# Reordering the opening stage of a fused polynomial-sketch attention and SwiGLU kernel

## The chip, the cores and the metric

One core of a Trainium2 chip. The metric is device time in microseconds (us) of one execution. The five engines of the core run their own instruction lists in order: TensorE (PE in the profile; its weight loads are PEld), VectorE (DVE), ScalarE (ACT), GpSimd (POOL) and SyncE (SP, which only issues DMAs). A letter q behind an engine's name stands for its sequencer.

## The reference

Attention without softmax over 4 batches, 4 heads, 1088 positions, 32 values per head, then a SwiGLU block over the 4352 tokens:

```
phi(x) = outer(S1 x, S2 x)                 # 8 x 8 = 64 features per position
kv  = sum over s of phi(k) v               # 64 x 32 per head
z   = sum over s of phi(k)                 # 64 per head
attn = (phi(q) kv) / (phi(q) z + 1e-6)
x    = attn, heads side by side            # 4352 x 128
out  = (silu(x w_gate) * (x w_val)) w_out  # d_ff = 1536
```

q, k and v are float32. [...]

## The kernel before

**The long part.** x is kept transposed in SBUF, 128 features by 4352 tokens, cut into 12 blocks of 384 or 320 tokens (three per batch). A *unit* (L646) is one block against one of 12 slices of 128 hidden columns: two matmuls (gate and value, L651), a silu on ACT (L657) and a product on DVE (L665). `down` (L673) is the third matmul (L679). Units fill the span from about 17 us to the end, and the attention of later batches is slipped in between them.

**The opening.** Before the first unit, the attention of batch 0 has to give the first block of x, and the first slices of the weights have to be narrowed. The order of every engine's instructions is the order of the lines in the source; nothing reorders them. The opening is L720 to L844:

- Loads. SP issues S1, k (544 KB), the first third of q, four pieces of v, later the second third of q, the second pieces of the gate and value weights, and the last third of q. ACT issues S2 and the first weight pieces. I call the pieces of the gate weights wg0 (128 columns), wg1 (256 columns), wg2 and so on, those of the value weights wv0, wv1, wv2. The DMAs take eight completion semaphores in turn, in the order of the source. A DMA whose semaphore still belongs to an earlier DMA first waits, on its engine, for that earlier one to land. So the fourth piece of v waits for k, as the two share a semaphore.
- Sketches. `s12` and `sq` (L755 to L762) are S1 and S2 laid out for the matmuls.
- Keys. `turn_k` transposes k on DVE in three pieces (L263), `key_products` (L278) multiplies with S1 and S2, `key_copy` brings a product from PSUM to SBUF on ACT (L295, or L292 for the last piece), and `key_features` (L301) forms the 64 features `phk`. The first two pieces' features are made by DVE, the last one's by POOL.
- `unit_sums` (L324) adds the features over the positions (z, then `zq`), `key_values` (L312) multiplies them with v (kv, then `kvs`). `turn_sums` (L343) and `turn_kv` (L335) turn both round into `kvz`.
- Queries, by thirds of the batch (`steps`): `turn_q` (L269), `query_products` (L368), `query_copy` on ACT (L384, L387), `query_features` on DVE (L398, L404; one instruction where a product has a two-bank buffer, two where it has two single banks).
- `totals` (L420) gives denominators (`which=(1,)`) and numerators (`which=(0,)`), `divide` (L433) transposes the denominators (`dT`, L441), inverts them (`rc`), spreads them (`rd`, L449) and writes x (`xT`, L466).
- Narrowing. `narrow` (L199) works in three steps, which `part(name, i)` calls one at a time: L217 and L218 on DVE; L222 and L223 on ACT; L225 and L229 on DVE followed by a multiplication on POOL (L238; of wg1 and wv1, half of it on DVE), and then the issue of a further weight load by SP. Four raw buffers hold 64-bit pieces, so a further load waits until the raw data of an earlier piece has been read.
- `keep_warm` (L189) runs matmuls without use for their result, to keep PE busy.

PSUM has four single banks, g0, g1, g2 and acc, and two two-bank buffers, a and b.

Of the kernel before, what the change touches and what calls it, by code (L numbers as in the profile page):

```python
# [19 lines left out]
def kernel(  # L20
# [28 lines left out]
    nc = tc.nc  # L49
    P = nc.NUM_PARTITIONS  # L50
    B, H, S, Dh = q.shape
# [3 lines left out]
    NX = S // 32  # L55
    HX = NX // 2
    NC = (NX + 3) // 4
    F = R * R
# [7 lines left out]
    XS = plan[0]  # L66
# [21 lines left out]
    def bank(tag=None):  # L88
        if tag is None:
            tag = free_banks[turn[0] % len(free_banks)]  # L90
            turn[0] += 1
        return psum.tile([P, TB], FP32, tag=tag, name="bank")

    def wide(tag):
        return psum.tile([P, 2, TB], FP32, tag=tag, name=tag)
# [6 lines left out]
    wide_w = moe_w_gate.dtype == I64  # L102
# [12 lines left out]
    NRAW = 4  # L115
# [6 lines left out]
    def load_q(b, x0=0, x1=NX):  # L122
        src = q[b].rearrange("h (pp x) d -> (h pp) x d", pp=32)
        nc.sync.dma_start(out=qld[:, x0:x1, :], in_=src[:, x0:x1, :])
# [14 lines left out]
    def load_next(queue=nc.sync):  # L139
        if not coming:  # L140
            return
        name, i = coming.pop(0)
        dst, src = weights[name]
        c0, c1 = pieces[name][i]
        if name == "wo":
            part = src.rearrange("(c p) d -> p c d", p=P)[:, c0:c1, :]
        else:
            part = src.rearrange("p (c f) -> p c f", f=P)[:, c0:c1, :]
        if not wide_w:
            queue.dma_start(out=dst[:, c0:c1, :], in_=part)  # L150
            return
        t = raw[name, i] = stage.tile([P, 3, P], I64, tag="raw", name="raw", bufs=NRAW)
        queue.dma_start(out=t[:, 0 : c1 - c0, :], in_=part)
# [114 lines left out]
    def turn_q(x0, n):  # L268
        nc.vector.transpose(  # L269
            out=qT[:, 2 * x0 : 2 * x0 + 2 * n, :],  # L270
            in_=qld[:, 2 * x0 : 2 * x0 + 2 * n, :],
        )
# [13 lines left out]
    def key_copy(ps, c0, c1, aside=False):  # L286

        n = c1 - c0
        ab = ps[:, 0 : 64 * n].rearrange("p (x t r) -> p x t r", t=2, r=R)
        if aside:  # L290
            kab = apool.tile([P, n * H, 2, R], FP32, tag="kab", name="kab")
            nc.scalar.copy(kab[:], ab)  # L292
            return kab[:, :, 0, :], kab[:, :, 1, :]
        ka = apool.tile([P, n * H, R], FP32, tag="ka%d" % c0, name="ka")
        nc.scalar.copy(ka[:], ab[:, :, 0, :])  # L295
        return ka[:], ab[:, :, 1, :]

    def key_features(phk, prod, c0, c1, engine=nc.vector):
        ka, kb = prod
        n = (c1 - c0) * H  # L300
        engine.tensor_tensor(  # L301
            out=phk[:, c0:c1, :, :, :].rearrange("p c h i j -> p (c h) i j"),
            in0=ka.unsqueeze(3).to_broadcast([P, n, R, R]),
            in1=kb.unsqueeze(2).to_broadcast([P, n, R, R]),
            op=ALU.mult,
        )

    def key_values(kv, phk, c0, c1):

        for c in range(c0, c1):  # L310
            for h in range(H):
                nc.tensor.matmul(  # L312
                    kv[32 * h : 32 * h + 32, 0:F],
                    vld[:, h, c, :],
                    phk[:, c, h, :, :].rearrange("p i j -> p (i j)"),
                    start=(c == 0),
                    stop=(c == NC - 1),
                )

    def unit_sums(kz, phk, c0, c1):  # L320

        for c in range(c0, c1):
            a = c % 4
            nc.tensor.matmul(  # L324
                kz[32 * a : 32 * a + 32, 0 : H * F],
                ones[:, 0:Dh],
                phk[:, c, :, :, :].rearrange("p h i j -> p (h i j)"),
                start=(c < 4),
                stop=(c + 4 >= NC),
            )  # L330

    def turn_kv(kvs, kzp):
# [18 lines left out]
    def query_products(x0, n, tags):  # L351

        w = 32 * n
        pss = []
        for pr in range(2):
            if isinstance(tags[pr], str):
                both = wide(tags[pr])[:].rearrange("p g (t w) -> p g t w", t=2)
                parts = [both[:, g] for g in range(2)]
            else:
                both = None  # L360
                parts = [
                    bank(t)[:].rearrange("p (t w) -> p t w", t=2) for t in tags[pr]
                ]
            for t in range(2):
                for half in range(2):
                    for g in range(2):
                        r = slice(64 * pr + 32 * g, 64 * pr + 32 * g + 32)
                        nc.tensor.matmul(  # L368
                            parts[g][F * half : F * half + F, t, 0:w],
                            sq[r, t, :, :].rearrange("p i j -> p (i j)"),  # L370
                            qT[r, 2 * x0 : 2 * x0 + 2 * n, :].rearrange(
                                "p (x a) t -> p a x t", a=2
                            )[:, half],
                            start=True,
                            stop=True,
                        )
            pss.append((both, parts))
        return pss

    def query_copy(n, both, parts):  # L380
        w = 32 * n
        qb = apool.tile([P, 2, 32 * XS], FP32, tag="qb", name="qb", bufs=2)
        if both is not None:
            nc.scalar.copy(qb[:, :, 0:w], both[:, :, 1, 0:w])  # L384
        else:
            for g in range(2):
                nc.scalar.copy(qb[:, g, 0:w], parts[g][:, 1, 0:w])  # L387
        return qb
# [40 lines left out]
    def side_by_side(tag):  # L429
        both = wide(tag)[:].rearrange("p g (t w) -> p g t w", t=2)  # L430
        return both[:, :, 0, :], both[:, :, 1, :]
# [292 lines left out]
    def part(name, i):  # L724

        next(fills[name, i], None)
# [3 lines left out]
    if wide_s:  # L730
# [1 line left out]
        steps_s = narrow(s32[:], sraw[:], [2 * R, Dh])  # L732
        next(steps_s)
        next(steps_s)
    for _ in range(2):
        load_next(nc.scalar)
    load_q(0, 2 * XS, 4 * XS)
    for _ in range(2, NRAW if wide_w else len(coming) + 2):
        load_next()
    load_q(0, 4 * XS, NX)  # L740
    run(steps_s)
    srep = bank("g0")
    for h in range(H):
# [16 lines left out]
    )  # L760
    nc.scalar.copy(sq[:, 0, :, :], sTv[:, 0, :].unsqueeze(2).to_broadcast([P, R, R]))
    nc.scalar.copy(sq[:, 1, :, :], sTv[:, 1, :].unsqueeze(1).to_broadcast([P, R, R]))  # L762
    for c in fpieces:
        turn_k(*c)
    prods = []
    for t, c in zip(("g1", "g2", "acc"), fpieces):
        ps = bank(t)
        key_products(ps, *c)
        prods.append(key_copy(ps, *c, aside=(c[1] == NC)))
    phk = apool.tile([P, NC, H, R, R], FP32, tag="phk", name="phk")  # L770
    kz, kv = bank("g0")[:, 0 : H * F], wide("b")[:, 0, 0:F]
    n = steps[0][1]
    key_features(phk, prods[0], *fpieces[0])
    unit_sums(kz, phk, *fpieces[0])
    turn_q(*steps[0])
    pss = query_products(*steps[0], ("a", ("g1", "acc")))
    qbs = [query_copy(n, *pss[0])]
    key_features(phk, prods[1], *fpieces[1])
    unit_sums(kz, phk, *fpieces[1])
    key_features(phk, prods[2], *fpieces[2], engine=nc.gpsimd)  # L780
    unit_sums(kz, phk, *fpieces[2])
    part("wg", 0)
    part("wv", 0)
    zq = apool.tile([P, H * F], FP32, tag="zq", name="zq")
    kvs = apool.tile([P, F], FP32, name="kvs0")
    kvz = [apool.tile([P, P], FP32, name=x) for x in ("kvz0", "kvz1")]
    qbs.append(query_copy(n, *pss[1]))
    nc.scalar.copy(zq[:], kz)
    key_values(kv, phk, *fpieces[0])
    phq = query_features(n, pss, qbs, pairs=(0,))  # L790
    query_features(n, pss, qbs, phq=phq, pairs=(1,))
    turn_q(*steps[1])
    ps = bank("g0")
    turn_sums(zq, sel[:], ps)
    nc.scalar.copy(kvz[1][:], ps[:, 0:P])
    part("wg", 0)
    key_values(kv, phk, *fpieces[1])
    nd = [bank(t) for t in ("g2", "acc")], side_by_side("a")[0]
    totals(n, phq, kvz, nd, which=(1,))
    key_values(kv, phk, *fpieces[2])  # L800
    nc.scalar.copy(kvs[:], kv)
    ps = bank("g1")
    turn_kv(kvs[:], ps)
    nc.scalar.copy(kvz[0][:], ps[:, 0:P])
    part("wv", 0)
    totals(n, phq, kvz, nd, which=(0,))
    pss = query_products(*steps[1], ("b", ("g0", "g1")))
    qbs = [query_copy(steps[1][1], *ps) for ps in pss]
    turn[0] = 2
    keep_warm(3, ps=wide("a")[:, 0, :])  # L810
    divide(0, *steps[0], nd, among=("wg", "wv"))

    att = attention(1, ((0, 3), (3, NC)))
    for _ in range(2):
        part("wg", 1)
        part("wv", 1)
    unit(0, 0, late=True)
    phq = query_features(steps[1][1], pss, qbs)  # L820
    part("wg", 1)
    part("wv", 1)
    nd = totals(steps[1][1], phq, kvz, side_by_side("b"))
    unit(0, 1, late=True)
    divide(0, *steps[1], nd)
    part("wg", 2)
# [113 lines left out]
```

## Time and profile before

| | us |
|---|---|
| median of 4 runs (lowest, highest) | 311.71 (311.44, 312.49) |
| the profiled execution's own time | 311.97 |
| its span in the profile | 310.2 |
| PE busy in the span | 302.5 |
| DVE / ACT / POOL busy | 176.3 / 96.0 / 37.2 |

Busy time by stage, us:

| stage | length | PE | DVE | ACT | POOL |
|---|---|---|---|---|---|
| 0 to 6.40 | 6.40 | 4.73 | 1.57 | 2.05 | 2.46 |
| 6.40 to 16.89 | 10.49 | 9.18 | 8.90 | 4.51 | 2.34 |
| 16.89 to 25 | 8.11 | 7.49 | 7.90 | 5.11 | 1.21 |
| 25 to 35 | 10.00 | 10.00 | 7.90 | 7.61 | 4.92 |
| 35 to 60 | 25.00 | 24.83 | 23.72 | 13.21 | 9.11 |
| 60 to 300 | 240.00 | 240.00 | 124.48 | 62.57 | 17.13 |

The profile shows one execution. A row of its timeline gives the start, the length, the engine, the line, what is written from what, and in brackets how long the engine had been idle and what ended that. The chain of waits goes back from the last instruction to what released each step; its rows give start, length and what ran. Busy time of PE is modelled at its matmuls' ends, and successive instructions of an engine overlap by some hundredths of a us, so that steps are best counted from start to start.

### The profile page before, as it was taken

To read this page: it belongs to the slowest core of one execution; us is meant where nothing else is said; L and a number is where in the kernel's file an instruction comes from. 1 tells how busy PE (TensorE), PEld (TensorE's weight loads), DVE (VectorE), ACT (ScalarE), POOL (GpSimd) and SP (SyncE) were. 2 spreads that over 40 slices of the span, in tenths; PEclk is the share of its full clock that TensorE was granted. 3 is DMA by queue.
4 is the path that set the end of the run, shared out by engine and by line. 5 is a ranking of instruction groups with operands and counts; after the bars stand their busy time and mean duration, and the time that the engine had idled before them with its cause. 6 is when DMAs were issued, how large, how long until landed. Compare 5 with 4: busy or idle time off the path is not lost.

```text
span 310.2 us, 5154 instructions
## 1 busy us (share of the span) xinstructions
PE 302.5 (97%) x2068; PEld 191.0 (62%) x2068; DVE 176.3 (57%) x333; ACT 96.0 (31%) x228; POOL 37.2 (12%) x54
## 2 busy tenths in 40 slices
PE   7899999999999999999999999999999999999994
PEld 6445555656565556666666666655676656676664
DVE  3797999752758655369944552897522323333321
ACT  3457666232102223132222232222222222222230
POOL 3225322335000001500000033000000000000000
PEclk9999999999999999999999999999999999999998
DMA  7564291402211021120100100100010100100101
GB/s 189 138 184 121 63 311 45 146 0 56 44 27 21 2 97 49 25 74 0 26 2 0 22 3 2 19 6 0 8 20 0 21 2 1 25 0 1 23 0 25
DMA packets 24663, 13.96 MB, mean 45 GB/s; under 512 B 18368, under 2 KB 22720, under 8 KB 24640
## 3 DMA queue, kind: packets, MB, share of 16 engines
q1 hardware_dynamic: 23712, 13.28, 16.9%
q10 hardware_dynamic: 928, 0.36, 0.6%
q8 instruction: 16, 0.26, 0.4%
q14 instruction: 7, 0.06, 0.1%
HBM read 11.41 MB, written 2.23 MB: 44 GB/s over the span
## 4 chain that ended last, share of the span: by engine, by line
PE 87%; DVE 7%; ACT 2%; DMA 1%; issue 1%; SPq 0%; DVEq 0%
PE bank L651 50%; PE bank L679 28%; DVE hj L665 2%; DMA kld<-in_k_dram 1%; DVE exp L225 1%; PE a L602 1%; PE a L278 1%; PE a L312 1%; PE b L278 1%; DVE exp L217 1%; DVE man L229 1%; PE a L693 1%; PE a L528 1%; ACT exp L222 1%; PE bank L324 1%
## 5 line engine op out<-in xcount | busy, mean ns | idle before, releaser
L665 DVE TENSOR_TENSOR hj<-sg,bank 128x384 f32<-128x384 f32 (+1 forms) x138 | 72.7, 529 | 102.3 <-PE bank L651 101.3
L657 ACT ACTIVATE sg<-bank 128x384 f32<-128x384 f32 (+1 forms) x144 | 67.7, 472 | 155.9 <-PE bank L651 155.8
L651 PE MATMUL bank<-xT,wg 128*128 128x384 f32 (+1 forms) x288 | 112.9, 474 | 0.2 <-DVE wg L238 0.2
L651 PE MATMUL bank<-xT,wv 128*128 128x384 f32 (+1 forms) x288 | 111.6, 469 | 0.4 <-DVE wv L238 0.4
L679 PE MATMUL bank<-hj,wo 128*128 128x384 f32 (+2 forms) x288 | 105.3, 460 | 0.2 <-DVE hj L665 0.2
L651 PEld LDWEIGHTS bank<-xT,wv 128*128 128x128 f32 x288 | 54.2, 190 | 34.5 <-DVE hj L665 2.6
L679 PEld LDWEIGHTS bank<-hj,wo 128*128 128x128 f32 x288 | 54.4, 190 | 32.9 <-issue 0.8
L651 PEld LDWEIGHTS bank<-xT,wg 128*128 128x128 f32 x288 | 53.1, 190 | 32.0 <-issue 2.6
L474 POOL TENSOR_TENSOR zs<-phk 128x1024 f32<-128x1024 f32 x3 | 7.1, 2352 | 111.9 <-PE bank L651 104.2
L565 DVE TENSOR_REDUCE dot<-phq 128x96 f32<-128x768 f32 x9 | 13.8, 1532 | 0.0
L301 DVE TENSOR_TENSOR phk<-kas,a 128x512 f32<-128x512 f32 (+1 forms) x12 | 8.7, 749 | 5.2 <-ACT kas L509 5.2
L707 DVE STREAM_TRANSPOSE o<-bank 128x384 f32<-128x384 f32 (+2 forms) x12 | 6.6, 549 | 6.9 <-PE bank L679 6.6
L222 ACT ACTIVATE exp<-exp,rebias 128x384 int32<-128x384 int32 (+3 forms) x15 | 8.3, 555 | 4.9 <-DVE exp L217 4.2
L589 DVE STREAM_TRANSPOSE phT<-phq 128x768 f32<-128x768 f32 x9 | 8.7, 968 | 0.1
L301 DVE TENSOR_TENSOR phq<-qab 128x768 f32<-128x768 f32 x9 | 8.6, 951 | 0.0
L558 DVE TENSOR_TENSOR phq<-zrep,qab 128x768 f32<-128x768 f32 x9 | 8.5, 942 | 0.0
L225 DVE SCALAR_TENSOR_TENSOR exp<-raw,exp 128x384 int32<-128x384 int32 (+2 forms) x14 | 7.7, 547 | 0.0
L620 ACT COPY xT<-a 128x64 f32<-128x64 f32 (+4 forms) x9 | 2.4, 332 | 15.9 <-PE b L602 9.5
L217 DVE TENSOR_SCALAR exp<-raw 128x384 int32<-128x384 int32 (+2 forms) x14 | 6.6, 474 | 0.6 <-DMA raw<-in_moe_w_val_dram 0.6
L229 DVE SCALAR_TENSOR_TENSOR man<-raw,man 128x384 f32<-128x384 uint32 (+2 forms) x14 | 6.9, 491 | 0.0
L223 ACT ACTIVATE man<-man 128x384 f32<-128x384 int32 (+3 forms) x15 | 6.8, 453 | 0.0
L263 DVE STREAM_TRANSPOSE kT<-kld 128x384 f32<-128x384 f32 (+2 forms) x9 | 6.1, 692 | 0.7 <-DMA kld<-in_k_dram 0.7
(113 smaller groups left out, 162.7 us busy)
## 6 DMA issues: line engine op xcount, KB each, us to landing
kld<-in_k_dram SPq DMA_DIRECT2D x4, 544.0 KB, 4.5
vld<-in_v_dram SPq DMA_DIRECT2D x12, 144.0 KB, 5.2
qld<-in_q_dram SPq DMA_DIRECT2D x3, 544.0 KB, 3.3
raw<-in_moe_w_out_dram SPq DMA_DIRECT2D x4, 384.0 KB, 4.2
out_dram<-o SPq DMA_DIRECT2D x28, 48.0 KB, 1.8
raw<-in_moe_w_gate_dram SPq DMA_DIRECT2D x3, 384.0 KB, 3.2
raw<-in_moe_w_val_dram SPq DMA_DIRECT2D x3, 384.0 KB, 3.2
out_dram<-o SPq DMA_DIRECT2D x16, 40.0 KB, 1.7
```

What stands on the lines that cost most here:

```text
L217: nc.vector.tensor_scalar(e[:], hi, 0x7FF00000, None, op0=ALU.bitwise_and)
L222: nc.scalar.activation(e[:], e[:], AF.Relu, bias=rebias[: shape[0], :], scale=8.0)
L225: nc.vector.scalar_tensor_tensor(out=e[:], in0=hi, scalar=-(1 << 31), in1=e[:], op0=ALU.bitwise_and, op1=ALU.bitwise_or,)
L229: nc.vector.scalar_tensor_tensor(out=f, in0=lo, scalar=2.0**-52, in1=f, op0=ALU.mult, op1=ALU.add)
L301: engine.tensor_tensor(out=phk[:, c0:c1, :, :, :].rearrange("p c h i j -> p (c h) i j"), in0=ka.unsqueeze(3).to_broadcast([P, n, R, R]), i ...
L558: nc.vector.tensor_tensor(out=prod, in0=zrep[:].unsqueeze(1).to_broadcast([P, n, H * R, R]), in1=fac.unsqueeze(3).to_broadcast([P, n, H * ...
L565: nc.vector.tensor_reduce(out=dot[:, x, :], in_=phq[:, c0:c1, :, :, :].rearrange("p c h i j -> p (c h) j i"), axis=AX.X, op=ALU.add,)
L589: nc.vector.transpose(out=phT[:, :, :, c0:c1, :].rearrange("p h g c t -> p c (h g) t"), in_=phq[:, c0:c1, :, :, :].rearrange("p c h (g i) ...
L651: nc.tensor.matmul(o[:, 0:n], w[:, j, :], xT[:, t0 : t0 + n], start=True, stop=True)
L657: nc.scalar.activation(sg[:, 0:n], g[:, 0:n], AF.Silu)
L665: nc.vector.tensor_tensor(out=hj[:, 0:n], in0=sg[:, 0:n], in1=u[:, 0:n], op=ALU.mult)
L679: nc.tensor.matmul(acc[i][:, 0:n], wo[:, j, :], hidden[i, j][:, 0:n], start=(j == 0), stop=(j == NCH - 1),)
```

## The change

Only the opening is changed. Of the three pieces of keys, POOL's (now called `aside`) is transposed, multiplied and copied first, and its features are added as the second of the three. The first third's query products come right behind the key products on PE, into the two two-bank buffers a and b, and the transpose of that third of q goes ahead of the key features on DVE; the query features follow the key features. kv is gathered in the single bank acc, in the order first, POOL's, second piece. The two weight loads of ACT are issued behind its copies of the sketches, and they and the rest of the loads come later in the source, so that the eight semaphores are dealt out anew: of the four pieces of v none waits for another DMA any more, the second third of q waits for S2 as before, and the load of wv0 now waits for k. The first narrowing step of wg1 comes ahead of `divide`, its last step ahead of the query features of the second third, and the first step of wv1 behind them. `keep_warm(3)` becomes `keep_warm(1)`. From `part("wg", 2)` on, the instructions are the same.

```diff
@@ key_values, unit_sums @@
-    def key_values(kv, phk, c0, c1):
+    def key_values(kv, phk, c0, c1, order=range(NC)):
...
-                    start=(c == 0),
-                    stop=(c == NC - 1),
+                    start=(c == order[0]),
+                    stop=(c == order[-1]),
...
-    def unit_sums(kz, phk, c0, c1):
+    def unit_sums(kz, phk, c0, c1, order):
...
             a = c % 4
+            same = [x for x in order if x % 4 == a]
...
-                start=(c < 4),
-                stop=(c + 4 >= NC),
+                start=(c == same[0]),
+                stop=(c == same[-1]),
@@ the opening @@
-    for _ in range(2):
-        load_next(nc.scalar)
-    load_q(0, 2 * XS, 4 * XS)
-    for _ in range(2, NRAW if wide_w else len(coming) + 2):
-        load_next()
-    load_q(0, 4 * XS, NX)
     run(steps_s)
...
     nc.scalar.copy(sq[:, 1, :, :], sTv[:, 1, :].unsqueeze(1).to_broadcast([P, R, R]))
-    for c in fpieces:
+    for _ in range(2):
+        load_next(nc.scalar)
+    load_q(0, 2 * XS, 4 * XS)
+    for _ in range(2, NRAW if wide_w else len(coming) + 2):
+        load_next()
+    load_q(0, 4 * XS, NX)
+
+    c0, c1, aside = fpieces
+    order = [c for p in (c0, aside, c1) for c in range(*p)]
+    for c in (aside, c0, c1):
         turn_k(*c)
-    prods = []
-    for t, c in zip(("g1", "g2", "acc"), fpieces):
+    prods = {}
+    for t, c in zip(("acc", "g1", "g2"), (aside, c0, c1)):
         ps = bank(t)
         key_products(ps, *c)
-        prods.append(key_copy(ps, *c, aside=(c[1] == NC)))
+        prods[c] = key_copy(ps, *c, aside=(c == aside))
+    turn_q(*steps[0])
+    n = steps[0][1]
+    pss = query_products(*steps[0], "ab")
+    qbs = [query_copy(n, *ps) for ps in pss]
     phk = apool.tile([P, NC, H, R, R], FP32, tag="phk", name="phk")
-    kz, kv = bank("g0")[:, 0 : H * F], wide("b")[:, 0, 0:F]
-    n = steps[0][1]
-    key_features(phk, prods[0], *fpieces[0])
-    unit_sums(kz, phk, *fpieces[0])
-    turn_q(*steps[0])
-    pss = query_products(*steps[0], ("a", ("g1", "acc")))
-    qbs = [query_copy(n, *pss[0])]
-    key_features(phk, prods[1], *fpieces[1])
-    unit_sums(kz, phk, *fpieces[1])
-    key_features(phk, prods[2], *fpieces[2], engine=nc.gpsimd)
-    unit_sums(kz, phk, *fpieces[2])
-    part("wg", 0)
-    part("wv", 0)
+    kz = bank("g0")[:, 0 : H * F]
+    key_features(phk, prods[aside], *aside, engine=nc.gpsimd)
+    for c in (c0, c1):
+        key_features(phk, prods[c], *c)
+    for c in (c0, aside, c1):
+        unit_sums(kz, phk, *c, order)
...
-    qbs.append(query_copy(n, *pss[1]))
     nc.scalar.copy(zq[:], kz)
-    key_values(kv, phk, *fpieces[0])
-    phq = query_features(n, pss, qbs, pairs=(0,))
-    query_features(n, pss, qbs, phq=phq, pairs=(1,))
+    kv = bank("acc")[:, 0:F]
+    key_values(kv, phk, *c0, order)
+    phq = query_features(n, pss, qbs)
+    part("wg", 0)
+    part("wv", 0)
     turn_q(*steps[1])
+    part("wg", 1)
     ps = bank("g0")
     turn_sums(zq, sel[:], ps)
     nc.scalar.copy(kvz[1][:], ps[:, 0:P])
     part("wg", 0)
-    key_values(kv, phk, *fpieces[1])
-    nd = [bank(t) for t in ("g2", "acc")], side_by_side("a")[0]
-    totals(n, phq, kvz, nd, which=(1,))
-    key_values(kv, phk, *fpieces[2])
+    key_values(kv, phk, *aside, order)
+    den = side_by_side("a")[0]
+    totals(n, phq, kvz, ([None] * 2, den), which=(1,))
+    key_values(kv, phk, *c1, order)
     nc.scalar.copy(kvs[:], kv)
...
     part("wv", 0)
+    part("wg", 1)
+    nd = [bank(t) for t in ("g2", "acc")], den
     totals(n, phq, kvz, nd, which=(0,))
...
-    keep_warm(3, ps=wide("a")[:, 0, :])
+    keep_warm(1, ps=wide("a")[:, 0, :])
     divide(0, *steps[0], nd, among=("wg", "wv"))
...
-    for _ in range(2):
-        part("wg", 1)
-        part("wv", 1)
     unit(0, 0, late=True)
+    part("wg", 1)
     phq = query_features(steps[1][1], pss, qbs)
-    part("wg", 1)
+    part("wv", 1)
     part("wv", 1)
     nd = totals(steps[1][1], phq, kvz, side_by_side("b"))
+    part("wv", 1)
     unit(0, 1, late=True)
```

## The prediction

> **What bounds the kernel.** First the page: PE is busy for nearly the whole span.
>
> ```profile
> PE 302.5 (97%) x2068; PEld 191.0 (62%) x2068; DVE 176.3 (57%) x333; ACT 96.0 (31%) x228; POOL 37.2 (12%) x54
> PE 87%; DVE 7%; ACT 2%; DMA 1%; issue 1%; SPq 0%; DVEq 0%
> ```
>
> What PE lacks to the span is 7.7 us, half of it at the end. So the opening can only win by letting PE begin its steady work earlier. Where it begins is read from the chain of waits of the first 30 us:
>
> ```profile
> 1.28 4.48 DMA kld<-in_k_dram
> 5.79 1.50 DVE kT L263 x3
> ...
> 10.89 0.18 issue
> 11.07 0.54 PE b L312 x24
> 11.61 0.59 PE bank L343 x16
> ...
> 15.43 0.60 DVE xT L466 x2
> ...
> 20.49 0.30 DVE wv L238
> 20.79 0.14 issue
> 20.93 3.69 PE bank L651 x10
> ```
>
> k lands at 5.76; PE and ACT carry the chain to 15.43; then DVE alone carries it to 20.79, and PE waits for the second slice of the value weights until 20.93. From there PE's units follow with few holes (10.00 busy of 10.00 in 25 to 35, 24.83 of 25 in 35 to 60). From `part("wg", 2)` on the instructions are the same, so what DVE's end of wv (20.79) gains, the whole rest should gain. DVE is nearly full too (23.72 of 25), but with the same work behind the same point it shifts as a whole.
>
> **Step 1, features.** The waits, of the engines and of SP's queue, tell why PE stood at 10.89 (who waited for whom, us in total, times, longest):
>
> ```profile
> PEld b L312 <- DMA vld<-in_v_dram: 0.6, 1, 0.6
> SPq L130 <- DMA kld<-in_k_dram: 2.2, 1, 2.2
> ```
>
> SP held the last piece of v for 2.2 us until k had landed, issued it at 5.78, and 5.2 later (page's landing for that form in the DMA view) it was there: 10.98. And the sums before it (L324) ended at 10.89, as POOL's features came last:
>
> ```profile
> 8.51 1.51 POOL L301 TENSOR_TENSOR phk<-kab 128x768 f32<-128x768 f32 x1 [4.86 <-ACT kab L292]
> 8.67 0.92 DVE L301 TENSOR_TENSOR phk<-ka,bank 128x768 f32<-128x768 f32 x1
> ```
>
> After: POOL's copy is ACT's first, 7.03 + 0.32, and POOL runs from about 7.51 to 9.02 instead of to 10.02. DVE does the same three instructions between 7.28 and the end of its features (transpose of q 0.57, features 0.95 and 0.92), only in another order: it ends at about 9.55, as now at 9.59. ACT's copies of the other products stay where PE's products put them (7.49, 8.03). PE's query products (0.93 from 8.97 to 9.90) fill 8.0 to 8.93, when PE now waits for features; their cover is that hole. Then the sums: two groups early, the last six matmuls at 9.55 + 0.15 for 0.63 (the first six of now, 8.41 to 9.04): 10.35 against 10.89. `zq` follows on ACT at 10.40 for 0.37, against 10.94; `turn_sums` (L343), which waits for it, starts at about 10.82 against 11.54: **-0.72**, if v lies there by about 10.3, so that the first `key_values` (0.47 to the next start) is out of the way. From there to `xT` PE and ACT do the same things (second and third group change places): `xT` starts at 15.41 - 0.72 = 14.69.
>
> **Step 2, DVE before `divide`.** `dT` could start at 13.27 - 0.72 = 12.55. DVE has 0.19 of room behind it (`rd` ends at 15.18, `xT` waits for PE to 15.41). In front of it now stand, behind the query features (two instructions of 0.55, the first from 9.47, when ACT has copied its product, so that they end at 10.49, where three end at 12.15 now): wg0's and wv0's first step, the transpose of q, and, new here, wg1's first step. From the landing of wv0 to `dT` that is 0.15 + 0.13 + 0.49 + 0.20 + 0.20 = 1.17 from start to start (rows of 10.79 to 12.07 and of 17.05 to 17.45). So wv0 must land by 12.55 + 0.19 - 1.17 = **11.57**, or DVE, whose list is in order, holds `dT`, and PE behind it, by what is over.
>
> **Step 3, loads.** wv0 lands at 10.77 now (issued by ACT at 3.19, 7.6 later). After the change ACT issues wg0 at 5.44 and wv0 at about 5.85, past k's landing, so that its new wait costs nothing; the kab copy behind it on ACT is not due before 7.03. SP issues v's last piece at about 3.6 instead of 5.78 and q's second third at about 4.1 instead of 6.13; wg1 and wv1 still wait for q's first third and v's first piece to land. The bytes are the same 2.46 MB, all landed by 12.99 now, so values win what weights lose. By the DMA view's stretches, 0.96 MB had moved by 5.8, 1.33 by 7.3, 1.54 by 8.4, 1.92 by 9.7, 2.28 by 11. k, q's first third and v are 1.31 MB: moved by 7.3. The last share of a transfer lands late (wv1: 2.3 MB moved at 11.05, landed at 8.37 + 4.2 = 12.57, so 1.5 behind): v lands at about 7.3 + 1.5 = 8.8, in time. wv0's turn: k, q, v, q's second third, wg0 and wv0 are 1.77 MB, 9.2 + 1.5 = 10.7 if nothing else comes between; with wg1 shared in, 10.1 + 1.5 = 11.6; with wv1 too, 12.6. The bounds are 10.7 and 12.6 (and 13.4, if it takes its 7.6 from issue again). I take 11.6, the middle, since now too SP's and ACT's transfers run side by side: of the stretch 5.8 to 7.3 the one queue had 54.9%, the other 53.5%. That is just in time.
>
> ```profile
> q1 hardware_dynamic: 349, 0.47, 85.0%
> q10 hardware_dynamic: 23, 0.02, 5.3%
> ```
>
> These two (4 to 5.8 us) show that ACT's loads, issued by 3.63, got next to nothing while SP's earlier ones were under way. The Trainium skill (DMA: Bandwidth & Descriptors, Queues, rings and completion order) says otherwise: each DMA engine goes round the queues packet by packet, so ACT's should have had a turn after one packet. By that rule wv0 would land near the lower bound and the sum stays as it is; by the row it stands behind what SP had queued, and up to 1.0 is lost.
>
> **Step 4, DVE from `xT` to wv.** From the start of `xT`'s second half to wv's end it is 20.78 - 15.69 = 5.09 now:
>
> ```profile
> 16.56 0.57 DVE L218 TENSOR_SCALAR man<-raw 128x256 int32<-128x256 int32 x1
> 19.43 0.69 DVE L225 SCALAR_TENSOR_TENSOR exp<-raw,exp 128x256 int32<-128x256 int32 x1
> ```
>
> Out of it goes wg1's first step (16.35 to 17.05, 0.70; the row of 0.57 is one that ran beside POOL's wv, against 0.28 alone). wv1's chain is now by itself: its first step comes behind the query features, so ACT's L222 and L223 (0.53 + 0.42) stand open between DVE's halves: DVE waits 0.5 for them. The row of 0.69 against 0.41 alone (POOL busy from 19.27) shows what POOL's multiplication costs a step beside it; one such meeting moves from wv1 to wg1, where POOL's wv now falls, and I charge it 0.17. Start to start: wv0 0.40, wg1 0.33 + 0.17 + 0.45 + 0.20, query features 1.00, wv1's first step 0.28, ACT 0.57, the last step 0.33 + 0.45 + 0.29, and 0.26 to begin with: 4.73. Step 4 gives **-0.36**. Bounds: -0.70 if ACT's part is hidden, +0.1 if POOL blocks two steps more.
>
> **Step 5, at nothing.** `keep_warm` loses two of three matmuls (0.82 together), PE's steps at 16.13 to 19.4 move up, but PE then waits for wv anyway, which is their cover; bare they would be worth 0.5. The granted clock is 1.00 in all stages to 300 us; nothing in these rows shows that 0.5 us of idle would lower it. The sums in another order and the bank of kv cost nothing: the same matmuls.
>
> **Sum.** -0.72 - 0.36 = -1.08. Against the execution's own 311.97 (span 310.2, 1.8 around it unchanged) that is 310.9; the median of the runs, 311.71, lies 0.26 lower: **310.6**. About 0.3% (0.94 us) is what a measurement can tell from no change here, so this stands at the edge.
>
> **Rivals.**
> (a) wv0 comes at 12.0 to 12.6: 0.4 to 1.0 of the gain go into DVE's wait ahead of `dT`. 311.1 to 311.7. For it: the 5.3% above. Against: ACT's loads ran evenly as soon as they had begun.
> (b) v is not earlier, as SP's and ACT's queues share the slow end as now: `key_values` starts at 11.07 again, only step 4 is left: 311.35.
> (c) Slower: ACT's loads keep their 7.6 from issue to landing. wv0 at 5.85 + 7.6 = 13.4 holds DVE 1.86 past its limit, and PE's numerators, x and all units with it: -1.08 + 1.86 = +0.78, 312.5. It decides from a landing at 12.65; 0.3% would need 13.6.
> (d) The front moves, but DVE, 95% busy in 35 to 60, gives it back: PE's holes there grow. About 311.7. Against: the same work stands behind the same point.
>
> **Numbers.** Forecast 0.43, (a) 0.25, (b) 0.14, (c) 0.08, (d) 0.10. The forecast's own spread is 310.2 (step 4 at its better bound) to 311.1; with (a), (b) and (d) and the unlike runs the range is 310.1 to 312.0, leaving out (c) and the tails. Faster by over 0.3%: most of the forecast's upper half and some more, 0.40; within 0.3%: (a), (b), (d) and the rest, 0.53; slower: part of (c), 0.07.
>
> **What would show it.** Right: `turn_sums` near 10.8, POOL's features ending near 9.0, `dT` near 12.6 without a DMA wait ahead of it, wv's L238 ending near 19.7, the first long run of L651 near 19.9. Wrong: a DVE wait for the raw weights ahead of the transpose of q (a, c), L312 waiting for v (b), or a front that is early at 20 and not at 60 us (d).

## The result and the profile after

The changed kernel takes **310.82 us** (median of 42 runs, 310.49 to 312.20; one more run, 312.35, is on record beside them), the kernel before 311.51 (64 runs, 311.26 to 313.04): a ratio of 0.9979, 95% interval 0.9973 to 0.9985, or 0.65 us less. That is inside the 0.94 us which the prediction called no change. The runs of every kernel here, this one and the one before alike, lie on two levels about 1 us apart (8 of these 42, and 11 of these 64, on the upper one; see the last section), so beside each ratio stands the **lower-level median**, over the runs within 0.8 us of the kernel's fastest: 310.78 after, 311.46 before, a difference of 0.68.

The profiled execution of after took 310.73 with a span of 309.0. Its page has PE as full as before:

```profile
PE 301.9 (98%) x2066; PEld 191.1 (62%) x2066; DVE 175.7 (57%) x332; ACT 96.2 (31%) x227; POOL 37.3 (12%) x54
PE 87%; DVE 7%; ACT 2%; DMA 1%; issue 1%; SPq 0%; DVEq 0%
```

The shares of the chain (second line) have not moved. PE is busy 0.6 less, as two dummy matmuls are gone, and the span is 1.2 shorter: the holes of the opening shrank. The chain of the first 30 us of after (start, us, what) shows where:

```profile
1.26 4.29 DMA kld<-in_k_dram
5.58 0.59 DVE kT L263
...
8.66 1.49 PE bank L325 x17
10.17 0.38 ACT zq L788
10.59 0.66 PE bank L344 x16
...
14.48 0.60 DVE xT L467 x2
...
19.32 0.30 DVE wv L238
19.62 0.14 issue
19.76 3.70 PE bank L652 x10
```

The wait for v (L312, at 11.07 before) is off the chain: the unit sums (L325) now run in one piece from 8.66, `zq` follows at 10.17, `turn_sums` (L344) stands at 10.59 instead of 11.54, and PE's long run of L652 begins at 19.76 instead of 20.93. From there on it is a plain shift: the first `hj` comes at 30.18 instead of 31.34 (-1.16), the hundred and first at 236.01 instead of 237.19 (-1.18).

So this pair of profiles shows 1.2 us and the runs 0.65. To settle that, each kernel was profiled once more (e10 and e11 below). The chain of the second profile of the kernel before:

```profile
1.28 4.30 DMA kld<-in_k_dram
5.61 1.50 DVE kT L263 x3
...
10.46 0.27 PE bank L324 x2
10.76 0.38 ACT zq L788
11.18 0.66 PE bank L343 x16
...
15.07 0.60 DVE xT L466 x2
...
20.13 0.30 DVE wv L238
20.43 0.14 issue
20.56 3.70 PE bank L651 x10
```

Compare it with the prediction's fence of the same kernel. There the sums ended at 10.89, v landed at 10.98 and L312 stood in the chain ahead of `turn_sums` at 11.54. Here v landed at 10.06, L312 no longer stands in the chain behind the sums (one of its matmuls, 0.06, shows among the last sums, whose rows on PE overlap with its own), `turn_sums` follows `zq` at 11.18, and PE's long run begins at 20.56. The own times were 311.97 and 311.59. The execution on which the prediction was made was thus a late one: of the 0.38 between the two, 0.18 is k's landing (5.76 against 5.58) and 0.18 what stood between k and `turn_sums` (5.78 against 5.60). Against this second profile the second profile of after gives -0.84 at wv's end (20.42 to 19.58), -0.87 at the hundred and first `hj`, and -0.77 in own time (310.82). That is near what the runs show.

### The profile page after: what moved, and what is told of

Its sections match the earlier page's. It is cut to its first block, busy times and chain, and to the rows that moved or that the text cites. A ratio compares the mean times of both kernels' runs of the same rounds, so it can differ in the third digit from the quotient of the medians.

```text
span 309.0 us, 5147 instructions
## 1 busy us (share of the span) xinstructions
PE 301.9 (98%) x2066; PEld 191.1 (62%) x2066; DVE 175.7 (57%) x332; ACT 96.2 (31%) x227; POOL 37.3 (12%) x54
## 4 chain that ended last, share of the span: by engine, by line
PE 87%; DVE 7%; ACT 2%; DMA 1%; issue 1%; SPq 0%; DVEq 0%
PE bank L652 50%; PE bank L680 28%; DVE hj L666 2%; DMA kld<-in_k_dram 1%; DVE exp L225 1%; PE a L603 1%; PE a L278 1%; PE a L312 1%; DVE man L229 1%; PE b L278 1%; DVE exp L217 1%; PE a L694 1%; ACT exp L222 1%; PE a L529 1%; PE bank L325 0%
## 5 line engine op out<-in xcount | busy, mean ns | idle before, releaser
L652 PE MATMUL bank<-xT,wg 128*128 128x384 f32 (+1 forms) x288 | 112.9, 474 | 0.0
L652 PE MATMUL bank<-xT,wv 128*128 128x384 f32 (+1 forms) x288 | 111.7, 469 | 0.3 <-DVE wv L238 0.3
L652 PEld LDWEIGHTS bank<-xT,wv 128*128 128x128 f32 x288 | 54.1, 190 | 34.6 <-DVE hj L666 2.6
L652 PEld LDWEIGHTS bank<-xT,wg 128*128 128x128 f32 x288 | 53.1, 190 | 31.5 <-issue 2.4
L222 ACT ACTIVATE exp<-exp,rebias 128x384 int32<-128x384 int32 (+3 forms) x15 | 8.3, 552 | 5.2 <-DVE exp L217 4.6
L229 DVE SCALAR_TENSOR_TENSOR man<-raw,man 128x384 f32<-128x384 uint32 (+2 forms) x14 | 7.2, 512 | 0.0
```

Of the source, the lines that this page charges most:

```text
L222: nc.scalar.activation(e[:], e[:], AF.Relu, bias=rebias[: shape[0], :], scale=8.0)
L229: nc.vector.scalar_tensor_tensor(out=f, in0=lo, scalar=2.0**-52, in1=f, op0=ALU.mult, op1=ALU.add)
L652: nc.tensor.matmul(o[:, 0:n], w[:, j, :], xT[:, t0 : t0 + n], start=True, stop=True)
```

## Experiments

*Narrowing* below means the steps (`narrow`) in which the kernel turns its 64-bit weights into float32. **The theory** after the result: two things gain, the front up to `turn_sums` (about 0.56, counted from k's landing in the second pair) and VectorE's order between `xT` and wv (0.22). The front needs both of its parts, since two arrivals meet there: the last features and v. **Rivals:** the earlier loads do it alone; POOL's order does it alone; the narrowing order does it all; or VectorE gives the gain back later. The table has all timed ones; "against before" is the difference from the lower-level median of the kernel before, timed beside it (before: 311.46, then 311.52 for e1 to e4, 311.57 for e5 to e8, 311.55 for e9).

| kernel | median, us | ratio, 95% interval | lower-level median | against before |
|---|---|---|---|---|
| after | 310.82 | 0.9979 (0.9973 to 0.9985) | 310.78 | -0.68 |
| e1 loads only | 311.74 | 1.0005 (0.9994 to 1.0016) | 311.71 | +0.19 |
| e2 loads back | 311.36 | 0.9992 (0.9980 to 1.0005) | 311.04 | -0.48 |
| e3 narrowing back | 311.00 | 0.9980 (0.9969 to 0.9992) | 310.96 | -0.56 |
| e4 POOL last | 311.52 | 0.9999 (0.9985 to 1.0013) | 311.02 | -0.50 |
| e5 three dummies | 310.81 | 0.9973 (0.9959 to 0.9988) | 310.71 | -0.86 |
| e6 wv1 early | 310.94 | 0.9980 (0.9966 to 0.9995) | 310.69 | -0.88 |
| e7 front only | 311.67 | 1.0001 (0.9989 to 1.0013) | 311.41 | -0.16 |
| e8 narrowing only | 311.53 | 0.9995 (0.9982 to 1.0007) | 311.30 | -0.27 |
| e9 fill | 310.82 | 0.9965 (0.9951 to 0.9979) | 310.81 | -0.74 |

The intervals are some 0.4 us to either side, and the lower-level medians of e1 to e9 rest on 6 to 11 runs each, so parts of 0.2 are not told apart by the runs alone; where a part is called shown, a stretch of the trace stands behind it.

**e1, the loads moved and nothing else** (kernel before; the same six lines, put behind the copies of the sketches):

```diff
-    for _ in range(2):
-        load_next(nc.scalar)
-    load_q(0, 2 * XS, 4 * XS)
...
     nc.scalar.copy(sq[:, 1, :, :], sTv[:, 1, :].unsqueeze(1).to_broadcast([P, R, R]))
+    for _ in range(2):
+        load_next(nc.scalar)
+    load_q(0, 2 * XS, 4 * XS)
```

> The kernel before, with the loads of the changed kernel and nothing else of it. Theory (front and narrowing order make the gain together, loads only allow it): POOL's features still end near 10.0 and the sums near 10.9, so only the 0.18 us for which PE waited for v can go: 0 to -0.2 us against before. Rival L (the earlier values make the gain): the whole -0.65 us of the runs. Rival D (only the narrowing order counts): 0.

No gain: 1.0005, and +0.19 by the lower level, where 0 to -0.2 was expected. The loads do not do it alone. v landed at 9.04, and L312 started only at 10.90, among the last sums, so v was not what came last. What came last this trace can't show: it is of an execution on the upper level, in which PE went from the query products (9.53) to the end of the sums (11.49) without a hole.

**e2, the loads back** in their old place, the rest as changed (the diff of e1 the other way round, on the kernel after):

> The changed kernel with the loads where they were. Theory: the last piece of v is issued when k has landed and lands near 10.9; key_values starts near 11.0 instead of 9.8, turn_sums near 11.4 instead of 10.6, so some 0.7 us of the gain go and the narrowing order's 0.2 to 0.3 stay: -0.2 against before. Rival L: gain gone, 0. Rival D: gain whole, -0.65.

-0.48 instead of -0.68: 0.2 to 0.26 of the gain goes, by the medians, and not the 0.45 that was expected. v landed at 10.38 there, 4.77 after k. Beside e8, which has the narrowing order alone (-0.27), the front without the loads is thus worth some 0.2, within the noise of both; e7 below says why it need not be nothing.

**e3, VectorE's narrowing order back**, the rest as changed:

```diff
-    part("wg", 1)
...
-    part("wg", 1)
...
     att = attention(1, ((0, 3), (3, NC)))
+    for _ in range(2):
+        part("wg", 1)
+        part("wv", 1)
     unit(0, 0, late=True)
-    part("wg", 1)
     phq = query_features(steps[1][1], pss, qbs)
-    part("wv", 1)
+    part("wg", 1)
     part("wv", 1)
     nd = totals(steps[1][1], phq, kvz, side_by_side("b"))
-    part("wv", 1)
```

> The changed kernel with the narrowing steps of wg1 and wv1 in the order of before (both first steps behind divide, both last steps behind the query features). Theory: xT is as early as in the changed kernel (14.5), the stretch from its second half to wv is 5.1 us again instead of 4.9: 0.2 to 0.36 us slower than the changed kernel, so -0.3 to -0.45 against before. Rival D: the gain is gone, 0. Rival L: no loss, -0.65.

-0.56 instead of -0.68. The trace is sharper than the time: from the start of `xT`'s second half to wv's end it takes 5.09 (16.05 to 21.15), as in both profiles of before, against 4.87 in both of after. The order is worth 0.22, no more.

**e4, POOL's third last again**, loads and narrowing as changed:

```diff
-    order = [c for p in (c0, aside, c1) for c in range(*p)]
-    for c in (aside, c0, c1):
+    order = [c for p in (c0, c1, aside) for c in range(*p)]
+    for c in (c0, c1, aside):
         turn_k(*c)
...
-    for t, c in zip(("acc", "g1", "g2"), (aside, c0, c1)):
+    for t, c in zip(("g1", "g2", "acc"), (c0, c1, aside)):
...
-    for c in (c0, aside, c1):
+    for c in (c0, c1, aside):
         unit_sums(kz, phk, *c, order)
```

> The changed kernel with POOL's third of the keys last in all places (transpose, product, copy, sums, values). Theory: POOL's features end near 9.9 instead of 8.9, the last group of sums near 10.6 instead of 10.15, turn_sums and all behind it 0.4 later: -0.25 against before. Rivals L and D: no loss, -0.65.

-0.50 by the lower level, where -0.25 was expected, and the median of all its runs is that of before, as 6 of its 12 runs lay on the upper level. So by these runs POOL's place is worth about 0.2 and not 0.4: with POOL last, this kernel still lies 0.23 below e8, and what it has besides e8's narrowing order is mainly the earlier loads and the query products ahead of the sums. The theory above leaves that second move out. In the kernel before, the sums did not wait for POOL alone:

```profile
9.83 1.06 PE L324 MATMUL bank<-phk,ones 128*32 128x256 f32 x12
```

The query products stood between the first six sums and these twelve, until 9.90, and the twelve ran in one piece; the first sum of POOL's piece came at 10.09, as POOL ended (10.01). PE's own list and POOL's features met there. No run moves the query products alone, so the front's 0.56 is not divided between them, POOL's place and the loads. The profile of this one, like those of e1, e2, e3 and e8, is of an execution on the upper level, in which the front is bound by something else (last section), so that it can't be read for POOL's part.

**e5, three dummy matmuls** instead of one:

```diff
-    keep_warm(1, ps=wide("a")[:, 0, :])
+    keep_warm(3, ps=wide("a")[:, 0, :])
```

> The changed kernel with keep_warm(3) back in front of unit(0, 0). Theory: PE waits for wv behind it anyway, so two matmuls of about 0.25 us more are hidden: no difference from the changed kernel, -0.65 against before. Rival (PE's order of the opening carries part of the gain): up to 0.5 slower than the changed kernel, -0.15.

310.71 against 310.78, and `xT` to wv 4.88 against 4.87: the two dummies cost nothing where PE waits anyway.

**e6, wv1's first step ahead of the query features** (kernel after):

```diff
+    part("wv", 1)
     phq = query_features(steps[1][1], pss, qbs)
-    part("wv", 1)
     part("wv", 1)
```

> The changed kernel with the first narrowing step of wv1 ahead of the query features instead of behind them, so that ACT's two steps run beside these. Theory: DVE's 0.37 us of waiting for ACT ahead of wv's last step go, wv ends 0.4 to 0.5 earlier, but the query features and with them PE's totals end 0.4 later, so PE comes to wv's matmul only at about 19.7 to 19.9: 0 to -0.1 against the changed kernel, -0.65 to -0.8 against before. Rival D (wv's end alone sets the start): -0.4 against the changed kernel, -1.1.

VectorE's stretch fell to 4.67 (15.21 to 19.88), as its wait for ACT's L222 went; yet the lower-level median is 310.69 against 310.78, which these runs can't tell from nothing. PE's totals of the second third of q ran from 18.41 to 19.78 and its first unit began right behind: at this point PE is the next bound.

**e7, the front only**: loads and narrowing as before, POOL's third and the query products as changed (the edits of e2 and e3 together).

> The changed kernel with both the loads and the narrowing order of before, so only POOL's third first, the query products behind the key products and the reordered features are left. If the parts add up as the first four kernels' runs have it (loads back cost 0.3 to 0.4, narrowing back 0.2): -0.1 to -0.2 against before. If the loads and the order only count together: 0. If the front is all: -0.65.

-0.16, a ratio of 1.0001: little or nothing. Its profile, of the lower level, shows what the front needs; the chain of its opening:

```profile
8.39 1.49 PE bank L325 x17
9.88 0.02 issue
9.90 0.38 ACT zq L787
10.28 0.14 issue
10.42 0.54 PE bank L312 x24
10.96 0.59 PE bank L344 x16
```

The sums are done at 9.85, 4.56 after k (5.29), as in the profile of after (10.12 - 5.55 = 4.57), but `key_values` (L312) starts only at 10.42, and `turn_sums`, behind it in PE's list, at 10.89. v had landed at 10.22. The trace names `zq` as what released L312, but in after, where v landed at 9.28, the same L312 started at 9.68, ahead of `zq` (10.17): it has no need of `zq`, and the wait was for v. From k's landing to `turn_sums` it is 5.60, that of the second profile of before, where the sums bound it: one late arrival was exchanged for another. With the loads moved as well it is 5.04 (both profiles of after). How late v comes varies: in the five profiles with the loads in their old place it landed 4.48 to 5.22 after k (e10 4.48, e8 4.73, e2 4.77, e7 4.93, before 5.22). At 4.93 nothing of the front's gain was left; with an earlier v some should be, which fits the 0.16 here and the 0.2 of e2, but no trace shows it.

**e8, the narrowing order only** (kernel before with the edit of e3 the other way round):

> The kernel before with the narrowing steps of wg1 and wv1 in the changed order and nothing else. Theory: wg1 lands at 11.3 to 11.9, in time for its first step before divide, so the stretch from xT to wv is 0.2 shorter as in the changed kernel: -0.2 against before. Rival (the order only helps with the early loads, as wg1 lands too late and holds dT): 0 or slower by up to 0.2.

-0.27, and `xT` to wv takes 4.88 against 5.09. These 0.21, the front's 0.56 and k's landing, 0.05 earlier in e11, make 0.82, near the 0.84 of the second pair of profiles.

**e9, PE's hole ahead of the key products filled** (e6, and):

```diff
-    keep_warm(16, 32, ps=ps)
+    keep_warm(30, 32, ps=ps)
```

> The changed kernel with wv1's first step ahead of the query features (as in the run before with that one edit) and 14 more narrow dummy matmuls behind the 16 that stand between the sketches and the key products, so that PE has work in most of the 0.7 us that it now waits for kT (14 x 0.03 to 0.06 us). Theory A (runs come on two levels about 1.2 us apart because PE's full pace begins either by 6 or only at 10 us, and this hole decides which): hardly any run on the upper level, the median of all runs at the lower level's 310.7, the mean 0.2 to 0.3 us less than the changed kernel's. Theory B (when the full pace begins is not set by this hole): about one run in five on the upper level as before; median 310.7 to 310.9, as without the fill. Against both: if the dummies are still running when kT is ready, everything behind shifts by up to 0.3 us: 311.0.

310.81 at the lower level, with 1 of 12 runs on the upper one. Against 8 of 42 that is too few runs to say that the hole matters (at 8 in 42, 12 runs have one or none on it three times in ten). Inconclusive; it is not faster than the changed kernel where that is at its best.

**e10 and e11, both kernels once more**, without an edit, for the profiles used above:

> The kernel before, once more, for a second profile. Theory A (the first profile was of a slow sample, since k and v landed late in it): k lands at 5.3 to 5.6 and v's last piece by 10.4, turn_sums starts near 11.1 and wv ends near 20.2 to 20.4, own time near 311.4. Theory B (it was typical): k again at 5.7 to 5.8, v near 11.0, wv's end near 20.8, own time near 312.

> The changed kernel, once more, for a second profile: turn_sums near 10.6, wv's end at 19.5 to 19.7, own time near 310.7, if PE runs at full pace by 6 us; if its first matmuls run at half pace to 10 us, all of it 1.0 to 1.3 later.

k at 5.58, v at 10.06, `turn_sums` at 11.18, wv's end at 20.42, own time 311.59: the first profile of before was a late sample. After came out as before it: `turn_sums` 10.57, wv's end 19.58, own time 310.82.

## Why the prediction was right, and where its sizes were off

The mechanism held in the main, and 310.82 lies 0.2 above the forecast of 310.6. That it lies so near is partly luck: the forecast change was -1.1 and the measured one -0.7, but the 311.71 from which it was taken, a median of 4 runs, lay 0.20 above the 311.51 of 64. Two of its terms were too large, and two readings were wrong without harm.

**Step 1 (-0.72) should have been -0.56.** The side after was right to 0.02: k landed 0.21 earlier in the profile of after than in that of before, and with this taken out POOL's features ended at 9.09 (forecast 9.02), the sums at 10.33 (10.35, though its own terms add up to 10.33), and `turn_sums` stood at 10.80 (10.82). POOL's instruction of after:

```profile
7.38 1.50 POOL L301 TENSOR_TENSOR phk<-kab 128x768 f32<-128x768 f32 x1 [3.74 <-ACT kab L292]
```

The side before was wrong: 11.54 held 0.18 of a late v, which the second profile doesn't have (11.18 - 5.58 + 5.76 = 11.36, which is also what `zq`'s end at 10.94 + 0.37 and the 0.05 behind it give). The prediction had both rows in hand and took the difference from the wrong one. Its proviso, "if v lies there by about 10.3" (4.54 after k), was right: in e7 v came 4.93 after k, and the term was gone. Its reason, that POOL's features came last in the kernel before, names only one of two: PE's own list, with the query products between the sums, held the twelve last sums about as long, as they ran in one piece (see e4).

**Step 2 was right.** `dT` came at 12.32, 1.73 after `turn_sums`, as before (1.73). VectorE waited for wv0 ahead of the transpose of q, which the prediction had named as a sign of being wrong; it just had the room, so that sign was badly chosen:

```profile
10.99 0.23 DVE L217 TENSOR_SCALAR exp<-raw 128x128 int32<-128x128 int32 x1 [0.41 <-DMA raw<-in_moe_w_val_dram]
```

With a wait of 0.56 in the second profile `dT` still followed 1.72 behind.

**Step 3 was right in its result, for a wrong reason.** v landed at 9.28 (forecast 8.8), wv0 at 10.97 (11.6; in other kernels with these loads, 10.26 to 11.10). The row of 349 packets against 23 (4 to 5.8 us) was read as if ACT's queue had to stand behind what SP had queued. It shows something else: the queue had hardly begun. In the first profile of before, ACT's weight loads were issued from 2.78 on, and its queue q10 moved their first packet after 5.0, more than 2.2 later. Why it began so late no row shows. It did not wait for all that SP had queued before, as v's first piece, issued at 2.17, landed only at 8.35. From 5.5 to 7.5 the two shared about evenly. The DMA view of that kernel from 6.5 to 7 (packets, MB, share of 16 engines):

```profile
q1 hardware_dynamic: 53, 0.06, 57.3%
q10 hardware_dynamic: 55, 0.05, 52.5%
```

In after the start was about as late: issued from 5.07, none before 7.0. The sharing was less even: 67 packets of q10 against 39 of q1 from 7.5 to 8, then 191 against 297 from 8 to 10. The Trainium skill (DMA: Bandwidth & Descriptors, Queues, rings and completion order) has each engine go round the queues in turn. The even rows of before agree with that; the uneven ones of after don't show whether both queues had work on every engine. The lower bound of 10.7, which the prediction drew from it, was the better one. ACT's k wait cost nothing, as forecast: the kab copy was made at 6.91.

**Step 4 (-0.36) measured -0.22**: 5.09 in all five profiles with the old order (before, e1, e3, e7, e10), 4.87 to 4.88 in all six with the new one (after, e2, e4, e5, e8, e11). Term by term against the 4.73, from start to start: the open part of ACT was right (0.86 from wv1's first step to its last, forecast 0.85), and so were the query features (0.99, forecast 1.00). wg1's last step was not: 1.27 (15.40 to 16.67) instead of 1.15. The meeting with POOL, charged 0.17, cost about 0.27, all of it in one row, L229:

```profile
15.57 0.58 POOL L238 TENSOR_TENSOR wv<-man,exp 128x128 f32<-128x128 f32 x1 [1.76 <-DVE man L229]
...
15.74 0.68 DVE L229 SCALAR_TENSOR_TENSOR man<-raw,man 128x256 f32<-128x256 uint32 x1
...
16.46 0.29 DVE L238 TENSOR_TENSOR wg<-man,exp 128x128 f32<-128x128 f32 x1
16.50 0.56 POOL L238 TENSOR_TENSOR wg<-man,exp 128x128 f32<-128x128 f32 x1 [0.36 <-DVE man L229]
```

L229 takes 0.68 beside POOL's wv, against 0.42 at 18.87 without it. That is 0.10 of the 0.14 that step 4 fell short; the rest is hundredths here and there.

**Step 5 was right** (e5). **The sum:** -0.56 - 0.22 = -0.78, against -0.77 to -0.87 in the second pair of profiles and -0.65 to -0.69 in the runs.

**The rivals.** (a) fell: wv0 was at 10.97. (b) fell for this kernel, but it is what e7's profile shows: with v late the front is worth nothing. (c) fell: wv0 took 5.4 from issue, not 7.6. (d) fell: -1.17 at wv's end, -1.16 at the first `hj` and -1.18 at the hundred and first in the first pair; the shift was kept.

## What to carry to other kernels

Where two late arrivals meet at one instruction, moving either alone earns little: e1 and e7 gained nothing that their runs could tell, both together (e3) half a microsecond. Which arrivals meet is easily misnamed: here PE's own list, the query products ahead of the sums, stood beside POOL and v, and no run moved it alone. A gain of tenths is measured against one execution's chance landings, so before pricing it, take from the profile every other way to the same point (here `zq`'s end, 0.18 earlier than v's) and charge the smaller one. And a queue's share in a window says something of its turn only if its first packet lies before the window.

## What the runs showed of the hardware that was not expected

**PE's full pace begins early or late, and that is worth more than this change** (between the medians of the two levels lie 1.15 us in after and 0.96 in before). The first matmuls of after (profiled at the lower level), dummies and key products:

```profile
4.61 1.00 PE L195 MATMUL bank<-const-bfloat16-1.0 128*32 128x512 bf16 x18
...
6.30 1.40 PE L278 MATMUL bank<-s,kT 128*64 128x64 f32 x36 [0.70 <-DVE kT L263]
```

and the same matmuls in e1, profiled at the upper level:

```profile
4.66 1.46 PE L195 MATMUL bank<-const-bfloat16-1.0 128*32 128x512 bf16 x18
...
6.19 2.19 PE L278 MATMUL bank<-s,kT 128*64 128x64 f32 x36
```

The 36 key products take 2.19 instead of 1.40, and a unit-sum matmul about 0.61 instead of 0.38, up to about 10 us; then both run alike. The key products tell the two kinds apart, not the dummies, which took 1.46 and 1.43 in e5 and e6 too. All five profiles with slow key products (e1, e2, e3, e4, e8) are of runs on the upper level (own times 311.97 to 312.40), and none of the other eight is: after, e5, e6, e9 and e11 have 310.65 to 311.11, e7, e10 and before, in other orders, 311.37, 311.59 and 311.97. The granted clock in the page's row is 1.00 in all these stretches, so it has to be read from the durations of matmuls of one shape. The Trainium skill (TensorE: Matmul & The Clock Gate, Part 1: The HAM clock gate) tells of a half clock that is released some 4 us into sustained work, with run-to-run spread. The slow pace agrees in kind (here the matmuls took 1.6 times as long). PE's first dummies ran at 0.85; the early moment, by 6, fits the figure roughly, the late one, at about 10, does not. What decides between them is open (e9).

In such an execution the sums of the features are bound by PE: from k's landing to `turn_sums` it is 6.44 with the front changed (e3) and 6.42 with only the loads moved (e1), so the new front is worth nothing there.
